# Splitting one weight block over two DMA queues, loading three parameter rows instead of four, and dropping the joining block of a gated SSM and FFN kernel

## Chip, cores and metric

The kernel runs on one core of one Trainium2 chip. The metric is device time in microseconds of one execution, the median of three runs. Engines are named as the profile names them: PE (TensorE matmul, PEld its weight loads), DVE (VectorE), ACT (ScalarE), POOL (GpSimd), SP (SyncE). SP and ACT also issue DMA transfers; SPq and ACTq stand for these issuing instructions.

## The reference

One input x of 2048 rows by 448 columns goes through two branches, which a gate mixes row by row.

```
g   = sigmoid((x * gate_w).sum(-1))
A:    Lam_bar = exp(dt * (Lambda_re + i Lambda_im)),  dt = exp(log_dt)
      B_bar   = ((Lam_bar - 1) / Lam)[:, None] * (B_re + i B_im)
      h_t     = Lam_bar * h_(t-1) + B_bar x_t          (448 complex states)
      y       = 2 Re(C h) + x * Dskip
B:    out     = silu(x @ w1) @ w2                       (448 -> 1792 -> 448)
result = g * y + (1 - g) * out
```

Inputs and output are bfloat16. The parameters Lambda_re, Lambda_im and log_dt are rows of 448 values; the kernel needs them as columns, one value for each partition.

## The kernel before

**Tiles.** Rows of x are taken in pairs (even, odd). With the partition axis for x's columns, x is held transposed in XT: row blocks 0, 1 and 2 of 128 columns each, and a remainder of 64 columns as block 3. W1 lies in W1E in the same four row blocks; the first 768 of its columns come first (FA = 768), further columns later. A step of the first feed-forward product takes 512 even or odd rows and two 128-column blocks of W1 (fb and fb + 1), which fill two PSUM banks. PSUM has eight banks, taken in turn.

**An order written out by hand.** Each operation is handed to a Tracker with the names that it reads and writes. The Tracker appends it to the list of its engine, with waits on other engines' semaphores where needed. Each engine works through its own list strictly in order, so the order of the calls in the source is the order on each engine. DMA transfers are entries of SP's or ACT's list as well. At the end `emit` writes the lists out, inside `nc.Block()`: each engine branches to a block of its own, and at the block's end all engines wait for each other (line 1178 in the profile).

**The opening.** SP and ACT issue in turn (lines 276 to 294): the first half of the columns of XH (512 even rows of x, four pieces XA0 to XA3), W1's row block 0 in two column halves of 384, then on SP W1's row block 1 whole (768 columns, 192 KB), on ACT the second half of XH's columns (256 KB). Then come the four parameter rows, each one partition of R: log_dt and Lambda_re on SP, Lambda_im and Dskip on ACT. W1's row block 2 follows, then the remainder block in two pieces (`ld_wr`), then W1's later columns. SP waits for the two remainder pieces (`T.wait_all("sp", gE)`) before it issues the DMA transposes that bring the rest of x and the B matrices.

PE first runs 22 idle matmuls, then turns XH with `turn_x` (transposes by a matmul with the identity ID into banks 6 and 7). `turned_x` is DVE's copy into XT; the key `XTe0j` names it. `ffn1_first` is a generator that yields between matmuls: for six blocks of W1 (fb in the order 0, 2, 4, 1, 3, 5) it goes through row block 0 (in two halves of 256 rows), 1 and 2. Where it yields, other work for PE is put between. `ffn1_rem` adds the remainder block for two fb and lets ACT apply Silu (`ffn1_act`).

**From rows to columns.** `rd` lets DVE copy 64 columns of R, `mm_cols` turns R by four matmuls with four columns of ID, into bank 7, and DVE copies the result to PV: one column of partitions for each parameter row. DVE and ACT then compute columns from PV in turn (`pact` on ACT, `pts` and `ptt` on DVE): dt, the magnitude mag, the phase fractions phf, fr, f2, sine sn and cosine cs, and the decay factors lr, li, nli, lis, rr. f2 is what POOL and DVE need for the phase tables (`phases`, `phases2`); lr and its kin are needed by the scan of the states. Between the matmuls of row block 1, the columns stand after the second one, and the transposes of x blocks 2 and 3 after the fourth.

**The rest.** PE goes on through the feed-forward steps, the products with B, the second feed-forward product and the output product; DVE does the scans, ACT the activations. The last outputs leave through `yout`, and SP waits for all of them.

Of the kernel before, what the change touches and what calls it, by code (L numbers as in the profile page):

```python
# [7 lines left out]
ALU = mybir.AluOpType  # L8
# [11 lines left out]
D = 448  # L20
# [22 lines left out]
class Tracker:  # L43
# [92 lines left out]
                self.known[eng][g] = g.total  # L136
                self.ops[eng].append(("wait", g.sem, g.total))

    def emit(self, block):
        where = {"sp": block.sync, "act": block.scalar, "pool": block.gpsimd,  # L140
                 "dve": block.vector, "pe": block.tensor}
        for e in self.ENGINES:
            def body(eng, items=self.ops[e]):
                for it in items:
                    if it[0] == "wait":
                        eng.wait_ge(it[1], it[2])  # L146
                    else:
                        it[1](eng).then_inc(it[2], it[3])
            where[e](body)


def gated_mix(nc, A_x, A_Lambda_re, A_Lambda_im, A_B_re, A_B_im, A_C_re, A_C_im, A_log_dt,
              A_Dskip, B_x, B_w1, B_w2, gate_w, out):
    with ExitStack() as ctx:
        E = ctx.enter_context
        T = Tracker(nc, ctx)
# [65 lines left out]
        ps = E(nc.psum_tensor("ps", [128, 8, 512], F32))  # L222
# [13 lines left out]
        def swap_xr(eng, h, odd):  # L236
            hs = slice(h * 512, (h + 1) * 512)
            if odd:
                T.op(eng, lambda e: e.tensor_copy(XR[0:64, hs], XT[64:128, 7, hs]), reads=XO[h][1],
                     writes=[f"XR{h}b"])  # L240
            else:
                T.op(eng, lambda e: e.tensor_copy(XR[64:128, hs], XT[0:64, 3, hs]), reads=XE[h][1],
                     writes=[f"XR{h}a"])

        T.op("dve", lambda e: e.memset(R[:, :], 0.0), writes=["R0", "R1", "R2", "R3", "Rd"])
# [13 lines left out]
        def ld_w(eng, j, f0=0, f1=FA, key=""):  # L259
            ld(eng, W1E[:, j, f0:f1], B_w1[j * 128:(j + 1) * 128, f0:f1], f"W1Ej{j}{key}")  # L260
# [18 lines left out]
            ld_w(eng, 0, 384 * c, 384 * c + 384, c)  # L279
        for k, eng in ((2, "sp"), (3, "act")):  # L280
            ld(eng, XH[:, k, 0:256], x0[:, k, 0:256], XA[k])
        ld_w("sp", 1)
        ld("act", XH[:, :, 256:512], x0[:, :, 256:512], XA[4])
        for i, (eng, v) in enumerate((("sp", A_log_dt), ("sp", A_Lambda_re), ("act", A_Lambda_im), ("act", A_Dskip))):
            ld_row(eng, i, v)
        ld_w("sp", 2)
        gE = [ld_wr(eng, c, False) for c, eng in enumerate(("sp", "act"))]
# [22 lines left out]
        for i, src in enumerate((A_B_re, A_B_im)):  # L310
# [17 lines left out]
             writes=["IOTA"])  # L328
# [3 lines left out]
        SGN = ["SGa", "SGb"]  # L332
# [67 lines left out]

        def wj(fb):
            i, c = fb // 2, fb % 2
            return [f"W1Ej0{c}", "W1Ej1", "W1Ej2"] if i < 3 else ["W1Ed0", "W1Ed2"] if i < 5 else ["W1Ee0", "W1Ee1"]

        def w1(fb):
            return lambda p, j: W1E[p, j, ff(fb) * 128:(ff(fb) + 1) * 128] if j < 3 else \
# [17 lines left out]
        def ffn1_first():  # L424
            banks = [nxt() for _ in range(NF1)]
            for j, h in ((0, 0), (0, 1), (1, None), (2, None)):
                c = slice(0, 512) if h is None else slice(256 * h, 256 * h + 256)
                for n, fb in enumerate((0, 2, 4, 1, 3, 5)):
                    bank = banks[fb]
                    T.op("pe", lambda pe, fb=fb, bank=bank, j=j, h=h, c=c: pe.matmul(  # L430
                        ps[:, bank, c], W1E[:, j, ff(fb) * 128:(ff(fb) + 1) * 128], XT[:, j, c],
                        start=(h == 0), stop=(h == 0), skip_group_check=(h != 0)),
                        reads=[f"W1Ej{j}" if j else f"W1Ej0{fb % 2}"] + (
                            ["XTe02"] if j == 2 else [f"XTe0{j}{h}"] if h is not None else [f"XTe0{j}0", f"XTe0{j}1"]),
                        writes=[f"ps{bank}"])
                    if (j, h, n) in ((0, 0, 3), (0, 0, 5), (1, None, 1), (1, None, 3)):
                        yield
            yield banks

        def ffn1_rem(banks, fb):  # L440
            def mm(pe):
                ins = None
                for i, p in enumerate((LO, UP)):
                    ins = pe.matmul(ps[:, banks[fb + i], :], w1(fb + i)(p, 3), xh(0, 0, 3, p), start=False, stop=True,  # L444
                                    skip_group_check=True)
                return ins
            T.op("pe", mm, reads=rem_ffn1(0, 0, fb), writes=[f"ps{banks[fb]}", f"ps{banks[fb + 1]}"])
            ffn1_act(0, fb, banks[fb], 2)
# [11 lines left out]
                yield  # L460

        def rd():
            T.op("dve", lambda e: e.tensor_copy(R[0:4, D:512], R[0:4, 384:448]), reads=["R0", "R1", "R2", "R3"],  # L463
                 writes=["Rd"])

        def mm_cols(pe):
            ins = None
            for pt in range(4):
                ins = pe.matmul(ps[:, 7, pt * 8:pt * 8 + 4], R[:, pt * 128:(pt + 1) * 128],  # L469
                                ID[:, 0:4], start=True, stop=True)  # L470
            return ins
        ones = nc.const_aps.tensor(1.0, [128, 128], BF16)
# [13 lines left out]
        def turn_x(j, i):  # L486
            def mm(pe):
                ins = None
                for k in (2 * i, 2 * i + 1):
                    ins = pe.transpose(xp[j][:, k * 128:(k + 1) * 128], XH[:, k, j * 128:(j + 1) * 128], ID[:, :])  # L490
# [11 lines left out]
        first = ffn1_first()  # L502
# [5 lines left out]
        turned_x(1, 1)  # L508
        rd()
        next(first)  # L510
        T.op("pe", mm_cols, reads=["R0", "R1", "R2", "R3", "Rd", "ID"], writes=["ps7"])
        T.op("dve", lambda e: e.tensor_copy(
            PV[:, :, :], ps[:, 7, 0:32].rearrange("p (t c) -> p t c", c=8)[:, :, 0:4]),
            reads=["ps7"], writes=["PV"])
        next(first)

        names = {}

# [15 lines left out]
        def pts(o, a, s1, s2, op0, op1, ra):  # L534
            T.op("dve", lambda e: e.tensor_scalar(col(o), a, s1, s2, op0, op1), reads=ra, writes=[o])

        def ptt(o, a, b, op, ra):
            T.op("dve", lambda e: e.tensor_tensor(col(o), a, b, op), reads=ra, writes=[o])

        def pact(o, a, f, ra, scale=1.0, bias=0.0):  # L540
            T.op("act", lambda e: e.activation(col(o), a, f, bias=bias, scale=scale),
                 reads=ra, writes=[o])
# [3 lines left out]
            col("phf"), LIM, 1.0 / TWO_PI, col("dt"), ALU.mult, ALU.mult), reads=["PV", "dt"], writes=["phf"])  # L546
        ptt("ar", col("dt"), LRE, ALU.mult, ["dt", "PV"])
        pact("mag", col("ar"), AF.Exp, ["ar"])
        for j in (2, 3):
            for i in range(2):  # L550
                turn_x(j, i)
        for j in (2, 3):
            turned_x(j)
        T.op("dve", lambda e: e.tensor_copy(XR[64:128, 0:512], xp[3][0:64, :]), reads=["ps7"], writes=["XR0a"])
        T.op("act", lambda e: e.activation(JK[:, 0:1], HP[:, :], AF.Silu), reads=["HP"], writes=["JK0"])
        pts("phr", col("phf"), MAGIC, -MAGIC, ALU.add, ALU.add, ["phf"])
# [6 lines left out]
        T.op("dve", lambda e: e.scalar_tensor_tensor(  # L563
            c1("f2s", 3), c1("f2", 3), -1.0, SG[:, 0:1], ALU.mult, ALU.mult),
            reads=["f2"] + SGN, writes=["f2s"])
        pact("sn", col("fr"), AF.Sin, ["fr"], scale=SIN_SCALE)
        pact("cs", col("afr"), AF.Sin, ["afr", "HP"], scale=-SIN_SCALE, bias=HP[:, 0:1])
        ptt("lr", col("mag"), col("cs"), ALU.mult, ["mag", "cs"])
        ptt("li", col("mag"), col("sn"), ALU.mult, ["mag", "sn"])
        pts("nli", col("li"), -1.0, None, ALU.mult, ALU.bypass, ["li"])  # L570
        T.op("dve", lambda e: e.tensor_tensor(c1("lis", 3), c1("li", 3), SG[:, 0:1], ALU.mult),
             reads=["li"] + SGN, writes=["lis"])
        ptt("rr", col("mag"), col("mag"), ALU.mult, ["mag"])
        first = next(first)


        GP = (0, 0, 1, 1)
# [54 lines left out]
        def skip():  # L632
            for b in range(4):
# [8 lines left out]
        phases(0)  # L642
        phases(2, "dve")
        phases2(0)
        swap_xr("dve", 1, 0)
        phases2(2)
        phases(3)
# [2 lines left out]
             writes=["BTz"] + BTK[2:4])  # L650
# [393 lines left out]
            for _ in range(n):  # L1044
                nxt()

        for fb in (0, 2, 4):
            ffn1_rem(first, fb)
        pair(*ffn1_pair(0, NF1))
        run(ffn1(0, NF1 + 2))  # L1050
        late([ffn1_pair(1, 0)])
# [54 lines left out]
        f = ffn1(2)  # L1106
# [68 lines left out]
            yout(2 * kt + odd, bank, c)  # L1175
        T.wait_all("sp", outs)

        with nc.Block() as block:
            T.emit(block)


def bass_gated_mix__ssm_conv_s5__dense_activation_silu__prompt_kernel(nc, *args):
# [29 lines left out]
```

## Time and profile before

| what | value |
|---|---|
| median of 3 runs | 139.46 us (139.14 to 139.64) |
| the profiled execution's own time | 139.14 us |
| its span, first to last instruction | 137.0 us |
| PE, DVE, ACT busy | 132.8, 114.7, 93.7 us |
| PE's idle time in the opening, by releaser | 0.25 us W1E transfer, 0.38 us DVE's copy to R |
| granted TensorE clock | 1.0 |

The span is shorter than the execution's own time by 2.14 us, which lie before the first and after the last instruction. Times in the profile count from the first instruction. A line of the timeline gives the start, the length, the engine, the source line, the operation, the written and the read tile, and in brackets the idle time before it and what ended it. A matmul's length includes the time in which its results drain, so that lengths of neighbouring matmuls overlap; the distance between starts is what one costs. XT<-XN and the like name the written tile first. XN is the tile that XH is part of.

### The profile page before, as it was taken

Reading aid. Unit: us, or ns where it says so; the run is one execution under the profiler, and the core shown is the slowest. Engines: PE = TensorE matmul, PEld = TensorE weight load, DVE = VectorE, ACT = ScalarE, POOL = GpSimd, SP = SyncE. Lnnn points to the kernel's source line nnn. Section 1 sums busy time; section 2 is a strip of 40 time slices with the busy share of each in tenths; the row PEclk is TensorE's granted clock in tenths of the full one; section 3 lists DMA queues with packets and bytes.
Section 4 is the critical chain, followed back from the end, with each engine's and each line's share of the span. In section 5 each row is a group of like instructions: output and inputs, shape, how many; then the busy total and the mean of one; then the engine's idle time right before and its main releaser. Section 6 shows DMA issues by size and latency. Waiting matters only on the chain.

```text
span 137.0 us, 2417 instructions
## 1 busy us (share of the span) xinstructions
PE 132.8 (97%) x962; PEld 65.1 (48%) x963; DVE 114.7 (84%) x150; ACT 93.7 (68%) x146; POOL 15.3 (11%) x32
## 2 busy tenths in 40 slices
PE   7889999999999999999999999999999999999992
PEld 7444444444444554444445544445555555555551
DVE  1379999374699999999999999999999999990563
ACT  0369798899939994599997996797214437889200
POOL 7108179305000000000000000000000000000000
PEclk9999999999999999999999999999999999999999
DMA  4998949999999130000320000000000000232123
GB/s 112 264 282 168 170 83 164 146 189 370 384 194 139 36 75 0 5 0 0 77 62 20 0 0 0 5 0 0 0 0 0 0 5 20 80 101 67 67 101 101
DMA packets 24897, 11.94 MB, mean 87 GB/s; under 512 B 16564, under 2 KB 24376, under 8 KB 24888
## 3 DMA queue, kind: packets, MB, share of 16 engines
q1 hardware_dynamic: 23140, 10.76, 35.8%
q10 hardware_dynamic: 1748, 1.04, 2.6%
q8 instruction: 7, 0.11, 0.3%
q14 instruction: 2, 0.02, 0.0%
HBM read 5.51 MB, written 1.84 MB: 54 GB/s over the span
## 4 chain that ended last, share of the span: by engine, by line
PE 91%; DMA 3%; DVE 2%; ACTq 2%; issue 0%; DVEq 0%
PE ps L364 42%; PE ps L772 31%; PE ps L994 15%; DMA R<-in_A_Dskip_dram 3%; ACTq L227 2%; PE ps L430 2%; DVE HS L841 1%; DVE TMPS L1018 1%; PE ps L444 1%; PE ps L490 0%; PE ps L469 0%; DVE R L463 0%; DVEq L146 0%
## 5 line engine op out<-in xcount | busy, mean ns | idle before, releaser
L772 PE MATMUL ps<-W,AT 128*128 128x448 bf16 x224 | 42.9, 353 | 0.0
L364 PE MATMUL ps<-XT,W1E 64*128 64x512 bf16 x325 | 40.1, 376 | 0.0
L452 ACT ACTIVATE AT<-ps 128x1024 bf16<-128x1024 f32 x28 | 28.2, 1019 | 9.9 <-PE ps L364 9.8
L772 PEld LDWEIGHTS ps<-W,AT 128*128 128x128 bf16 x224 | 21.7, 98 | 21.2 <-issue 0.4
L364 PEld LDWEIGHTS ps<-XT,W1E 64*128 64x128 bf16 x325 | 16.5, 94 | 20.0 <-ACT VE L803 0.8
L364 PE MATMUL ps<-XT,BT 64*128 64x512 bf16 x156 | 20.2, 376 | 0.1
L785 ACT ACTIVATE BT<-ps,GT 128x448 bf16<-128x448 f32 x8 | 5.1, 633 | 13.1 <-PE ps L772 13.1
L364 PEld LDWEIGHTS ps<-XT,BT 64*128 64x128 bf16 x156 | 8.1, 94 | 9.6 <-DVE HS L841 0.6
L841 DVE SCALAR_TENSOR_TENSOR HS<-VE,P,ps 128x512 bf16<-128x512 bf16 (+1 forms) x13 | 9.6, 781 | 2.6 <-PE ps L364 2.3
L885 DVE TENSOR_TENSOR_SCAN G<-P,Q 128x1024 f32<-128x1024 f32 (+1 forms) x6 | 11.4, 1921 | 0.0
L994 PE MATMUL ps<-CO,VE 128*128 128x448 bf16 (+2 forms) x63 | 11.1, 332 | 0.0
L994 PE MATMUL ps<-CO,HS 128*128 128x448 bf16 x56 | 11.1, 352 | 0.0
L364 PE MATMUL ps<-XR,W1E 64*128 64x512 bf16 x25 | 9.2, 376 | 0.0
L994 PEld LDWEIGHTS ps<-CO,VE 128*128 128x128 bf16 x63 | 6.0, 98 | 4.8
L994 PEld LDWEIGHTS ps<-CO,HS 128*128 128x128 bf16 x56 | 5.5, 98 | 5.1
L838 DVE TENSOR_TENSOR Q<-G,COS 128x2048 bf16<-128x2048 f32 (+1 forms) x4 | 7.0, 1756 | 0.1
L838 DVE TENSOR_TENSOR Q<-G,SIN 128x2048 bf16<-128x2048 f32 (+1 forms) x4 | 7.0, 1752 | 0.0
L805 ACT ACTIVATE ps<-VE,P 128x1024 f32<-128x1024 bf16 x6 | 6.7, 1119 | 0.2
L841 DVE SCALAR_TENSOR_TENSOR VE<-HS,P,FP 128x512 bf16<-128x512 bf16 (+1 forms) x7 | 6.6, 977 | 0.1
L1018 DVE SCALAR_TENSOR_TENSOR OT<-ps,GT,BT 128x448 bf16<-128x448 f32 x4 | 2.6, 682 | 4.8 <-PE ps L994 4.8
L803 ACT ACTIVATE VE<-ps 128x1024 bf16<-128x1024 f32 x6 | 6.1, 1018 | 0.8 <-PE ps L364 0.8
L841 DVE SCALAR_TENSOR_TENSOR FP<-HS,P,VE 128x1024 f32<-128x1024 bf16 (+1 forms) x4 | 6.2, 1551 | 0.1
(120 smaller groups left out, 170.5 us busy)
## 6 DMA issues: line engine op xcount, KB each, us to landing
W<-in_B_w_dram SPq DMA_DIRECT2D x1, 1568.0 KB, 9.1
XN<-in_A_x_dram SPq DMA_DIRECT2D x1, 896.0 KB, 5.1
out_dram<-OT SPq DMA_DIRECT2D x8, 112.0 KB, 1.7
out_dram<-TMPS SPq DMA_DIRECT2D x7, 112.0 KB, 1.7
HS<-HS SPq DMA_DIRECT2D x4, 128.0 KB, 2.5
W1E<-in_B_w_dram SPq DMA_DIRECT2D x2, 192.0 KB, 4.1
XN<-in_A_x_dram SPq DMA_DIRECT2D x1, 384.0 KB, 5.9
XN<-in_A_x_dram ACTq DMA_DIRECT2D x1, 256.0 KB, 4.6
```

The source lines that it names most:

```text
L227: return T.dma(eng, lambda e: e.dma_start(dst, src), writes=[key], group=group)
L364: ins = pe.matmul(ps[:, bank, :], w(p, j), xh(odd, h, j, p), start=start and j == js[0], stop=stop and j == js[-1], skip_group_check=seeded)
L452: T.op("act", lambda e: e.activation(a[:, fb:fb + n, :], ps[:, bank:bank + n, :], AF.Silu), reads=[f"ps{bank + i}" for i in range(n)], wri ...
L772: ins = pe.matmul(ps[:, bank, 0:D], a[:, fb, q * 128:(q + 1) * 128], W2[:, ff(fb), :], start=(first and fb == 0), stop=(fb == NFB - 1), sk ...
L785: T.op("act", lambda e: e.activation(bs(tile), ps[:, bank, 0:D], AF.Copy, scale=sc), reads=[f"ps{bank}", "GT2" if h else "GRI"], writes=ks)
L803: T.op("act", lambda e: e.activation(VE[:, m:m + 2, hs], ps[:, b[0]:b[0] + 2, :], AF.Copy), reads=[f"ps{i}" for i in b], writes=vs)
L805: T.op("act", lambda e: e.activation(ps[:, o[0]:o[0] + 2, :], VE[:, m:m + 2, hs], AF.Copy, scale=c1("lr", pt)), reads=vs + ["lr"], writes= ...
L838: T.op("dve", lambda e: e.tensor_tensor(o, a, b, op), reads=reads, writes=writes)
L841: T.op("dve", lambda e: e.scalar_tensor_tensor(o, a, s, b, ALU.mult, ALU.add), reads=reads, writes=writes)
L885: T.op("dve", lambda e: e.tensor_tensor_scan(G[:, c, w], rb, Q1[:, c, w], init, ALU.mult, ALU.add), reads=[f"Q1{c}", "rr", f"G{c}"], write ...
L994: ins = pe.matmul(ps[:, bank, c], state(kt, odd, m), CO[:, m, c], start=False, stop=(m == YB[-1]), skip_group_check=True)
L1018: T.op("dve", lambda e: e.scalar_tensor_tensor(o, ps[:, bank, c], g, bs(tile)[:, c], ALU.mult, ALU.add), reads=[f"ps{bank}", "GT1_1", f"BS ...
```

## The change

The change has four parts.

- W1's second row block (j = 1) is loaded as two halves of 384 columns, one issued by SP and one by ACT, in the place where SP issued it whole. Matmuls wait for the half that they read. The generator now yields once in this block, after three matmuls (fb 0, 2, 4).
- Dskip's row is no longer loaded into R, so the parameter columns come from three rows. The column matmuls write to columns 256 and up of bank 7 under a name of their own (pv); DVE's copy to PV reads pv and ps7. The transposes of x blocks 2 and 3 follow directly, and DVE's copy of block 2 stands ahead of the parameter arithmetic.
- The remainder matmuls of fb 0, 2 and 4 with their Silu are moved up, so that on ACT sine and cosine stand behind the second Silu. The decay columns lr, li, nli and lis become `decays()`, called behind `phases2(0)`.
- `emit` writes the instructions without `nc.Block()`.

```diff
-    def emit(self, block):
-        where = {"sp": block.sync, "act": block.scalar, "pool": block.gpsimd,
-                 "dve": block.vector, "pe": block.tensor}
+    def emit(self):
+        nc = self.nc
+        where = {"sp": nc.sync, "act": nc.scalar, "pool": nc.gpsimd, "dve": nc.vector, "pe": nc.tensor}
         for e in self.ENGINES:
...
-        ld_w("sp", 1)
+        for c, eng in enumerate(("sp", "act")):
+            ld_w(eng, 1, 384 * c, 384 * c + 384, c)
         ld("act", XH[:, :, 256:512], x0[:, :, 256:512], XA[4])
-        for i, (eng, v) in enumerate((("sp", A_log_dt), ("sp", A_Lambda_re), ("act", A_Lambda_im), ("act", A_Dskip))):
+        for i, (eng, v) in enumerate((("sp", A_log_dt), ("sp", A_Lambda_re), ("act", A_Lambda_im))):
             ld_row(eng, i, v)
...
-                    if (j, h, n) in ((0, 0, 3), (0, 0, 5), (1, None, 1), (1, None, 3)):
+                    if (j, h, n) in ((0, 0, 3), (0, 0, 5), (1, None, 2)):
                         yield
...
-            T.op("dve", lambda e: e.tensor_copy(R[0:4, D:512], R[0:4, 384:448]), reads=["R0", "R1", "R2", "R3"],
+            T.op("dve", lambda e: e.tensor_copy(R[0:3, D:512], R[0:3, 384:448]), reads=["R0", "R1", "R2"],
                  writes=["Rd"])
...
-                ins = pe.matmul(ps[:, 7, pt * 8:pt * 8 + 4], R[:, pt * 128:(pt + 1) * 128],
+                ins = pe.matmul(ps[:, 7, 256 + pt * 8:260 + pt * 8], R[:, pt * 128:(pt + 1) * 128],
                                 ID[:, 0:4], start=True, stop=True)
...
-        T.op("pe", mm_cols, reads=["R0", "R1", "R2", "R3", "Rd", "ID"], writes=["ps7"])
+        T.op("pe", mm_cols, reads=["R0", "R1", "R2", "Rd", "ID"], writes=["pv"])
         T.op("dve", lambda e: e.tensor_copy(
-            PV[:, :, :], ps[:, 7, 0:32].rearrange("p (t c) -> p t c", c=8)[:, :, 0:4]),
-            reads=["ps7"], writes=["PV"])
-        next(first)
+            PV[:, :, :], ps[:, 7, 256:288].rearrange("p (t c) -> p t c", c=8)[:, :, 0:4]),
+            reads=["pv", "ps7"], writes=["PV"])
+        for j in (2, 3):
+            for i in range(2):
+                turn_x(j, i)
+        turned_x(2)
...
         pact("mag", col("ar"), AF.Exp, ["ar"])
-        for j in (2, 3):
-            for i in range(2):
-                turn_x(j, i)
-        for j in (2, 3):
-            turned_x(j)
+        turned_x(3)
...
+        first = next(first)
+        ffn1_rem(first, 0)
+        ffn1_rem(first, 2)
         pact("sn", col("fr"), AF.Sin, ["fr"], scale=SIN_SCALE)
         pact("cs", col("afr"), AF.Sin, ["afr", "HP"], scale=-SIN_SCALE, bias=HP[:, 0:1])
-        ptt("lr", col("mag"), col("cs"), ALU.mult, ["mag", "cs"])
-        ptt("li", col("mag"), col("sn"), ALU.mult, ["mag", "sn"])
-        pts("nli", col("li"), -1.0, None, ALU.mult, ALU.bypass, ["li"])
...
+        ffn1_rem(first, 4)
+
+        def decays():
+            ptt("lr", col("mag"), col("cs"), ALU.mult, ["mag", "cs"])
+            ptt("li", col("mag"), col("sn"), ALU.mult, ["mag", "sn"])
+            pts("nli", col("li"), -1.0, None, ALU.mult, ALU.bypass, ["li"])
...
         ptt("rr", col("mag"), col("mag"), ALU.mult, ["mag"])
-        first = next(first)
...
         phases(0)
         phases(2, "dve")
         phases2(0)
+        decays()
         swap_xr("dve", 1, 0)
...
-        for fb in (0, 2, 4):
-            ffn1_rem(first, fb)
         pair(*ffn1_pair(0, NF1))
...
-        with nc.Block() as block:
-            T.emit(block)
+        T.emit()
```

More of the change, by code (lines that the diff above doesn't have):

```diff
@@ L137, in wait_all @@
                 self.ops[eng].append(("wait", g.sem, g.total))
-    def emit(self, block):
-        where = {"sp": block.sync, "act": block.scalar, "pool": block.gpsimd,
-                 "dve": block.vector, "pe": block.tensor}
+    def emit(self):
+        nc = self.nc
+        where = {"sp": nc.sync, "act": nc.scalar, "pool": nc.gpsimd, "dve": nc.vector, "pe": nc.tensor}
         for e in self.ENGINES:
[L143 to L149, printed above, removed]
+            eng = where[e]
+            for it in self.ops[e]:
+                if it[0] == "wait":
+                    eng.wait_ge(it[1], it[2])
+                else:
+                    it[1](eng).then_inc(it[2], it[3])
 def gated_mix(nc, A_x, A_Lambda_re, A_Lambda_im, A_B_re, A_B_im, A_C_re, A_C_im, A_log_dt,
@@ L243, in swap_xr @@
                      writes=[f"XR{h}a"])
-        T.op("dve", lambda e: e.memset(R[:, :], 0.0), writes=["R0", "R1", "R2", "R3", "Rd"])
+        T.op("dve", lambda e: e.memset(R[:, :], 0.0), writes=["R0", "R1", "R2", "Rd"])
         T.op("dve", lambda e: e.memset(SG[0:64, 0:1], -1.0), writes=["SGa"])
@@ L402, in wj @@
             i, c = fb // 2, fb % 2
-            return [f"W1Ej0{c}", "W1Ej1", "W1Ej2"] if i < 3 else ["W1Ed0", "W1Ed2"] if i < 5 else ["W1Ee0", "W1Ee1"]
+            return [f"W1Ej0{c}", f"W1Ej1{c}", "W1Ej2"] if i < 3 else ["W1Ed0", "W1Ed2"] if i < 5 else ["W1Ee0", "W1Ee1"]
         def w1(fb):
@@ L432, in ffn1_first @@
                         start=(h == 0), stop=(h == 0), skip_group_check=(h != 0)),
-                        reads=[f"W1Ej{j}" if j else f"W1Ej0{fb % 2}"] + (
+                        reads=[f"W1Ej{j}" if j > 1 else f"W1Ej{j}{fb % 2}"] + (
                             ["XTe02"] if j == 2 else [f"XTe0{j}{h}"] if h is not None else [f"XTe0{j}0", f"XTe0{j}1"]),
                         writes=[f"ps{bank}"])
-                    if (j, h, n) in ((0, 0, 3), (0, 0, 5), (1, None, 1), (1, None, 3)):
+                    if (j, h, n) in ((0, 0, 3), (0, 0, 5), (1, None, 2)):
                         yield
@@ L565, in gated_mix @@
             reads=["f2"] + SGN, writes=["f2s"])
+        first = next(first)
+        ffn1_rem(first, 0)
+        ffn1_rem(first, 2)
         pact("sn", col("fr"), AF.Sin, ["fr"], scale=SIN_SCALE)
         pact("cs", col("afr"), AF.Sin, ["afr", "HP"], scale=-SIN_SCALE, bias=HP[:, 0:1])
-        ptt("lr", col("mag"), col("cs"), ALU.mult, ["mag", "cs"])
-        ptt("li", col("mag"), col("sn"), ALU.mult, ["mag", "sn"])
-        pts("nli", col("li"), -1.0, None, ALU.mult, ALU.bypass, ["li"])
-        T.op("dve", lambda e: e.tensor_tensor(c1("lis", 3), c1("li", 3), SG[:, 0:1], ALU.mult),
-             reads=["li"] + SGN, writes=["lis"])
+        ffn1_rem(first, 4)
[3 more added lines that the diff above has]
+            pts("nli", col("li"), -1.0, None, ALU.mult, ALU.bypass, ["li"])
+            T.op("dve", lambda e: e.tensor_tensor(c1("lis", 3), c1("li", 3), SG[:, 0:1], ALU.mult),
+                 reads=["li"] + SGN, writes=["lis"])
         ptt("rr", col("mag"), col("mag"), ALU.mult, ["mag"])
-        first = next(first)
         GP = (0, 0, 1, 1)
```

## The prediction

> **What bounds the kernel now.** I read the page first, then the busy time by stage, then PE's timeline of the opening, then the chain of waits, and last what the closing line of the program leaves behind. The page, busy time by engine:
>
> ```profile
> span 137.0 us, 2417 instructions
> ...
> PE 132.8 (97%) x962; PEld 65.1 (48%) x963; DVE 114.7 (84%) x150; ACT 93.7 (68%) x146; POOL 15.3 (11%) x32
> ```
>
> PE has some 4 us without work. The table by stage (length; busy time and instructions of each engine; clock; DMA share) says where:
>
> ```profile
> 0.00:3.90 3.90, 3.08 (x28) 2.87 (x28) 0.71 (x6) 0.00 (x0) 2.93 (x10) 1.00 0.50 124
> 3.90:10.10 6.20, 5.39 (x42) 2.84 (x43) 3.10 (x16) 3.48 (x7) 0.22 (x2) 1.00 0.99 282
> 10.10:31.40 21.30, 21.30 (x199) 9.56 (x200) 17.27 (x27) 18.89 (x20) 10.74 (x13) 1.00 0.93 160
> ...
> 33.00:134.00 101.00, 101.00 (x681) 49.07 (x682) 91.30 (x100) 70.02 (x118) 0.28 (x2) 1.00 0.23 54
> 134.00:137.00 3.00, 0.52 (x8) 0.31 (x5) 0.90 (x2) 0.00 (x0) 0.00 (x0) 1.00 0.27 81
> ```
>
> From 10.1 to 134 PE is full at full clock, so a change can move the time only by letting that stream begin earlier or later, by tearing a hole in it, or by shortening what follows it. The edits lie before 10.1 and after the last output. PE's timeline of the opening (start, length, last the idle time before):
>
> ```profile
> 5.11 0.83 PE L430 MATMUL ps<-XT,W1E 128*128 128x256 bf16 x6
> 6.19 0.61 PE L430 MATMUL ps<-XT,W1E 128*128 128x512 bf16 x2 [0.25 <-DMA W1E<-in_B_w_dram]
> 7.17 0.24 PE L469 MATMUL ps<-ID,R 128*128 128x4 bf16 x4 [0.38 <-DVE R L463]
> 7.49 0.38 PE L430 MATMUL ps<-XT,W1E 128*128 128x512 bf16 x1
> 7.71 0.61 PE L490 MATMUL ps<-ID,XN 128*128 128x128 bf16 x8
> 8.15 2.00 PE L430 MATMUL ps<-XT,W1E 128*128 128x512 bf16 x8
> ```
>
> Durations here include the pipeline's tail; I count starts. A 512-column matmul costs 0.215 us (starts at 10.09, 10.31, 10.53), a 256-column one 0.11, a transpose 0.055, the four column matmuls 0.1 together. So the six of row block 0 are done at 5.77 and PE is empty until 6.19: 0.42 us for W1's second row block. Two matmuls last to 6.62, and PE is empty until 7.17: 0.55 us for the parameter rows. Two more matmuls (7.27 to 7.70, one record is missing), eight transposes to 8.15, eight matmuls to 9.87; the remainder starts at 10.09, so another 0.22 us is lost, 0.12 of it before row block 2, whose transposed x is copied by DVE only from 8.13 to 8.55. The chain of waits agrees on which wait ends last:
>
> ```profile
> 3.33 3.44 DMA R<-in_A_Dskip_dram
> 6.78 0.04 DVEq L146
> 6.81 0.05 issue
> 6.86 0.18 DVE R L463
> 7.04 0.14 issue
> 7.17 0.24 PE ps L469 x4
> ```
>
> The binding event is the landing of the last parameter row at 6.77, and the column matmuls follow it by 0.40. The last view is the instructions of the line that closes the block:
>
> ```profile
> L1178 SPq COMPARE_BRANCH  x1: 33/33/33, 136.6 to 136.6; - x1
> L1178 SPq DRAIN  x1: 13/13/13, 136.8 to 136.8; - x1
> ...
> L1178 PEldq EVENT_SEMAPHORE  x1: 51/51/51, 136.9 to 136.9; - x1
> ```
>
> The last output is issued at 134.98 and takes 1.5 us, so it is there at about 136.5; the rest of the span, from 136.6 to 137.0, is branch, drain and the engines' mutual wait.
>
> **The change, part by part.**
>
> *No joining block.* Removed: the entry branch of each engine and, at the end, 136.6 to 137.0. The span loses 0.39 us if nothing takes its place; nothing hides it, since SP arrives last. The trace does not show what follows the span (139.14 against 137.0, so 2.14 us around it). Bounds: 0, if that time grows by what the span loses; 0.42, with some hundredths for the entry branches; no instruction is added that could make it a loss. I take 0.39, because the row shows it on the latest engine.
>
> *W1's second row block in halves.* The 192 KB piece is issued on SP at 2.17 and read by PE at 6.19. The halves are issued at 2.17 (SP) and 2.20 (ACT). Pieces of 96 KB took 2.4 and 2.6 us to land on these two queues, which gives 4.6 to 4.8; the latest I allow is the present 6.19. PE wants the first half at 5.77. Three matmuls instead of two now stand ahead of the column matmuls and need that half alone. By 4.8 they run from 5.77 to 6.42, by 6.19 to 6.84; both are before the column matmuls can start with the rows as they land now (7.17). So the 0.42 us wait disappears into the wait for the rows: alone this part moves one matmul, 0.215 us, ahead of the wait.
> The Trainium skill speaks against this part: DMA: Bandwidth & Descriptors, section "Issuing engines are not separate DMA queues", has transfers of all issuing engines interleave on the same 16 DMA engines, so a second queue saves only issue time. The DMA share of 0.99 from 3.9 to 10.1 agrees that there is no spare bandwidth; by that rule the half comes no sooner than 6.19, and the sum below would not change.
>
> *Three rows instead of four.* Dskip's row, the one that lands last, is gone, but Lambda_im stays on ACT and gets a new place: ahead of it are now XH1, W1's two halves, XH3 and the 256 KB of x (576 KB instead of 480 KB). ACT's issues cost 0.41 to 0.46 us each, so Lambda_im is issued at about 3.15, where it was 2.70 and Dskip 3.33. SP has 96 KB less ahead of its two rows. On both queues together the bytes ahead are the same 896 KB, on engines that are full. The nearest row is thus Dskip's landing: T = 6.77. Earlier bound: T = 6.02, below which PE is not free (6.42). Later bound: the 256 KB of x, issued at 2.66 instead of 2.20, land 4.6 us later (the page's figure for that transfer) at 7.26, and W1's third row block, issued at 3.30, passes them and the row as well (192 KB at the stage's 282 GB/s, 0.7 us): T = 7.95.
>
> *The order behind the columns.* Let M = max(6.42, T + 0.40) be the start of the column matmuls. Then 0.1 for them, four transposes of x column block 2 to M + 0.32. Block 3 shares bank 7 with the columns, and the copy to PV reads that bank: it starts 0.28 after M (7.45 against 7.17), lasts 0.18, and with about 0.07 for the signal PE goes on at M + 0.53 (a new stall of 0.21, where a matmul stood before). Four transposes to M + 0.75, three matmuls to M + 1.40, six of row block 2 to M + 2.69; DVE's copy for them, now ahead of the parameter arithmetic, ends at about M + 0.95, so the 0.12 goes. With the 0.10 before the remainder: M + 2.79, against 10.09 - 7.17 = 2.92 now. Gain 0.13 at T = 6.77; 0.88 at 6.02; a loss of 1.05 at 7.95. The time changes by T's change one to one.
>
> *Moves at no cost.* Sine and cosine behind two Silu: ACT's first Silu then waits only for PE; PE needs its banks 1.52 us after the remainder starts (11.61 against 10.09), and PE's own 0.22 plus tail 0.2 plus 1.0 of Silu leaves 0.1. Without the move the cosine (10.17 to 10.47) would hold it, at up to the front's gain. The four decay columns (0.9 + 3 x 0.15) behind the first phase table: first read by ACT at 26.5, ten us later. ACT's queue gets 0.45 of issuing and loses 0.24: its table load moves from 5.54 to 5.75, the Exp that needs it starts at 7.66, cover 0.6. SP issues as many transfers as before, but its six x transposes and the others begin when both remainder pieces of W1 have landed (7.88). If ACT's piece comes 0.2 later, all of them do, the copy at 28.14 too:
>
> ```profile
> DVE XR L239 <- DMA XT<-in_A_x_dram: 3.1, 1, 3.1
> ```
>
> It ends at 28.43 and PE reads it at 28.87: cover 0.3 less what the front gains, so 0 for the forecast and at most 0.2.
>
> **Sum.** 0.39 + 0.13 = 0.52. The profiled execution took 139.14, the fastest of three; the median is 139.46. Against its own time it gives 138.62, against the median 138.94. I predict the median. Differences within 0.3%, 0.42 us, are about what a measurement of this kernel can tell from no change.
>
> **Rivals.**
> - *One of the two gains fails.* Either the exit is only passed on to the time around the span (gain 0.13, 139.33), or the block's 0.39 is real and T is 6.95 (front -0.05, gain 0.34, 139.12), or the transposes take back 0.1 to 0.2. For it: the two gains lie just above 0.42 together, and each has zero within its bounds. Against it: the closing line's rows, and a row fewer to wait for. Middle 139.2.
> - *Lambda_im behind the large x transfer: slower.* PE's order is fixed, so row block 1's second half, all transposes and row block 2 are queued behind the column matmuls, and they behind the one row that lands last. Price: T beyond 6.77 one to one. From T = 7.29 on (6.77 + 0.13 + 0.39) it eats the whole gain; a T of 7.75 gives 139.46 - 0.52 + 0.98 = 139.92, the bound 7.95 gives 140.12. For it: the issue of x 0.46 later, and 96 KB more in front on that queue. Against it: SP's queue is that much lighter and engines serve both.
> - *The rows come early.* If T follows the SP rows' position, T is at or below 6.3 and the front gains 0.6 or more: 139.46 - 0.39 - 0.6 = 138.47. For it: Lambda_im stood ahead of Dskip on its queue and must have landed before it.
>
> **How the numbers follow.** Forecast 0.42, early rows 0.10, one gain failing 0.33, Lambda_im late 0.15. Faster by over 0.3% is the first two, 0.52; within it the third; slower the last. The range: low 138.5, near the early rows; high 139.6, past the middle rival and into the beginning of the late row, which leaves some 0.1 on either side. The likeliest case's own range is 138.7 to 139.04 (T from 6.5 to the point where the gain is 0.42).
>
> **What would show it.** Right: no instructions of the closing line after the last output, and a span that ends at its landing; the copy to R between 6.6 and 7.1, the first remainder matmul near 9.96, PE full from there, and no wait for W1 at row block 1. Wrong: a DVE wait before the copy to R that lasts past 7.3; a hole in PE at 28.9 with a DMA as its releaser; a hole at 11.6 before the banks of the first Silu; or the time around the span well over 2.14 us.

## The result and the profile after

The changed kernel takes 138.26 us (median of 15 runs, 137.78 to 139.60), the kernel before 139.29 in its own 15 runs (138.94 to 140.37). The ratio is 0.9937, with a 95% interval from 0.9912 to 0.9962: shorter, clear of noise, but by under 1%. Between the medians it is 1.03 us; by the ratio 0.88, with an interval from 0.53 to 1.23. The forecast was a gain of 0.52 and a time of 138.94 in a range from 138.5 to 139.6, so the direction was right and the time lies 0.24 us below the range. Of the 0.68 between 138.94 and 138.26, 0.17 is not the change's: the kernel before took 139.29 here and 139.46 in the three runs that the forecast started from. The profiled execution took 137.81 us, one of the two shortest of the 15; the profile of before, at 139.14, was near the low end too.

The head of its page and the busy time by engine:

```profile
span 136.3 us, 2407 instructions
...
PE 133.2 (98%) x962; PEld 66.0 (48%) x963; DVE 113.7 (83%) x150; ACT 93.5 (69%) x146; POOL 16.9 (12%) x32
```

Between the two profiled executions the span is 0.7 us shorter, but the time is 1.33 us shorter (139.14 to 137.81): what lies around the span went from 2.14 to 1.51 us. That is where the forecast missed. The table by stage (length; busy time and instructions by engine in the order PE, PEld, DVE, ACT, POOL; clock; DMA share) shows the stream behind the opening as it was, without a hole:

```profile
3.90:10.10 6.20, 6.08 (x42) 3.71 (x44) 3.24 (x17) 3.39 (x6) 0.22 (x2) 1.00 0.93 277
10.10:31.40 21.30, 21.30 (x200) 9.51 (x198) 16.31 (x25) 18.93 (x21) 12.97 (x16) 1.00 0.91 171
```

PE's timeline of the opening (start, length; no line carries a wait):

```profile
5.67 1.67 PE L430 MATMUL ps<-XT,W1E 128*128 128x256 bf16 x9
7.18 0.24 PE L469 MATMUL ps<-ID,R 128*128 128x4 bf16 x4
7.28 0.81 PE L490 MATMUL ps<-ID,XN 128*128 128x128 bf16 x8
8.14 1.89 PE L430 MATMUL ps<-XT,W1E 128*128 128x512 bf16 x8
9.96 0.39 PE L444 MATMUL ps<-XT,W1E 64*128 64x512 bf16 x1
```

The first matmul of the remainder starts at 9.96, exactly where the forecast put it, but by another way. The rows had landed early: DVE copies them at 6.12 (the forecast: 6.6 to 7.1).

```profile
6.12 0.16 DVE L463 COPY R<-R 3x64 bf16<-3x64 bf16 x1
```

PE could not use it. The same four 256-column matmuls start at 4.01 in both profiles; the transposes behind them start at 4.45 before and at 4.82 after:

```profile
4.01 0.60 PE L430 MATMUL ps<-XT,W1E 128*128 128x256 bf16 x4
4.45 0.28 PE L490 MATMUL ps<-ID,XN 128*128 128x128 bf16 x2
```

```profile
4.01 1.01 PE L430 MATMUL ps<-XT,W1E 128*128 128x256 bf16 x4
4.82 0.42 PE L490 MATMUL ps<-ID,XN 128*128 128x128 bf16 x2
```

From start to start a 256-column matmul takes 0.21 us in the changed kernel, from 4.2 until about 6.1, and 0.11 behind that; in the kernel before it takes 0.11 from 4.01 on. So PE ran at half rate until about 6 here. The clock column of the stage table reads 1.00 in both profiles all the same; the half rate is read from the starts. So row block 0 ended at 6.53 instead of 5.77, and the column matmuls, behind three more matmuls, began at 7.18, limited by PE. An early landing and a slow PE cancelled: that the remainder began at 9.96 is luck. The chain that ended last has this stretch so:

```profile
5.88 1.46 PE ps L430 x9
7.34 0.08 PE ps L469 x4
7.42 0.24 PE ps L490 x4
7.67 0.02 issue
7.69 0.40 PE ps L490 x4
```

The piece from 7.42 to 7.69 is the stall at bank 7: the fifth transpose starts 0.24 after the start of the fourth, where 0.055 is usual.

At the end, the last output lands at 136.25 and the span ends at 136.30. Before, it landed at 136.52, and branch, drain and the mutual wait lasted to 136.99. So within the span the closing line cost 0.47, and 0.05 is left of it: 0.42 us, the upper bound of the forecast.

### The profile page after: what moved, and what is told of

It reads as the page before. It is cut to its first block, busy times and chain, and to the rows that moved or that the text cites. A ratio compares the mean times of both kernels' runs of the same rounds, so it can differ in the third digit from the quotient of the medians.

```text
span 136.3 us, 2407 instructions
## 1 busy us (share of the span) xinstructions
PE 133.2 (98%) x962; PEld 66.0 (48%) x963; DVE 113.7 (83%) x150; ACT 93.5 (69%) x146; POOL 16.9 (12%) x32
## 4 chain that ended last, share of the span: by engine, by line
PE 96%; DVE 2%; issue 0%; DVEq 0%
PE ps L364 43%; PE ps L778 31%; PE ps L1000 15%; PE ps L430 4%; PE ps L478 2%; PE ps L490 1%; DVE HS L847 1%; DVE TMPS L1024 1%; PE ps L444 1%; PE ps L469 0%; DVEq L146 0%
```

## Experiments

In all sixteen kernels the sixteen transfers that transpose x, B and C on their way are replaced by plain transfers of the same bytes from about 7.9 us on: that transposition is left out, and other values reach the later matmuls. Everything that the change touches is kept. The time around the span is a run's time less the span of that same run, which is on record to 0.1 us; medians are over all runs, ranges in brackets. "Ratio to before" compares with runs of the real kernel before on the same chip.

### What the joining block is worth

Four kernels: both openings, each with and without the block.

```
plain_block:    before, plain transfers        plain_noblock: the same, with
-        with nc.Block() as block:             plain_opening: changed opening, block kept
-            T.emit(block)                     plain_after:   changed kernel, plain transfers
+        T.emit()
```

> The kernel before, in which the 16 transposing transfers (of x, B and C, from 7.9 us on) are plain transfers of as many bytes into the same tiles; so x, B and C lie untransposed there and the values are others. It is the base of the following kernels, which all have plain transfers. Both theories: within 0.4 us of before, since PE is the bound from 10.1 us on and these transfers begin only when the opening is nearly over; 2.1 us around the span.

> The base with one edit: the instructions are written without the joining block. Theory 1 (the joining block is dearer than its 0.39 us in the span, because the time around the span falls too, from 2.14 to 1.5): about 1.0 us faster than the base, with 1.5 us around the span. Theory 2 (the block is worth its 0.39 us, and the rest of the gain comes from parameter rows that land early): 0.4 us faster, with 2.1 us around the span.

> The opening of the changed kernel, with the joining block left in, and plain transfers. Theory 1: within 0.3 us of the base, 2.1 us around the span. Theory 2: 0.6 us faster than the base.

> The changed kernel with plain transfers, on the chip of the other three. Both theories: 0.9 to 1.1 us faster than the base. In its profile, theory 1 has the moment at which matmuls go from 0.107 to 0.055 us each (3.9 us in the run of before, 5.9 in that of after) at another place again, and the remainders starting earlier or later by up to 0.9 us with it.

| kernel | time, us | span | around | ratio to before [95%] |
|---|---|---|---|---|
| plain_block | 138.89 (138.51 to 139.31) | 137.05 | 1.90 | 0.9935 [0.9906, 0.9965] |
| plain_noblock | 138.11 (137.73 to 138.48) | 136.6 | 1.50 | 0.9874 [0.9827, 0.9922] |
| plain_opening | 138.56 (138.26 to 138.94) | 136.6 | 2.02 | 0.9904 [0.9871, 0.9937] |
| plain_after | 137.88 (137.61 to 138.05) | 136.35 | 1.54 | 0.9858 [0.9806, 0.9910] |

From plain_block to plain_after it is 1.01 us, as between the two real kernels (1.03), so the stand-ins carry the effect. The block is worth 0.78 with the old opening and 0.68 with the new one, and the runs of neither pair overlap. The opening is worth 0.33 with the block and 0.23 without it, but there the runs of both pairs overlap. The forecast had 0.39 and 0.13. The time around the span falls by 0.40 and 0.48 when the block goes: the half that the forecast did not have. The plain transfers alone take the kernel before from 139.77 on that chip to 138.89, more than the 0.4 that I had allowed.

### What of the block costs time outside the span

First the mutual wait without the branches:

```
+        nc.all_engine_barrier()      # after T.emit(), in the changed kernel
```

> The changed kernel with plain transfers and one mutual wait of all engines at the end, but without the block's branches. So far the block costs 0.4 us in the span and about 0.5 us in the time around it. Theory A (the mutual wait is what is paid for, in both places): 0.6 to 0.9 us slower than plain_after_2, with 1.9 to 2.1 us around the span. Theory B (the branches pay for the time around the span): the span grows by 0.2 to 0.4 us, the time around it stays at 1.5, 0.2 to 0.4 slower.

> The changed kernel with plain transfers once more, the common measure of this set. The copy to R starts in its profile where the last parameter row lands; this was 6.12 in the run of after and 6.99 in plain_after. If the landing is as loose as that, it lies somewhere between 6.0 and 7.2 again, and the remainders start 2.8 us after the column matmuls whatever it is.

It gives the gain back: 138.71 (138.38 to 139.03, ratio 0.9929 [0.9907, 0.9950]) against 137.87 (137.72 to 137.93) for the changed kernel on another chip, with 2.08 around the span against 1.52. So outside the span it is the wait of the engines for each other and not the branches. Inside it, 0.30 us lie between the last output's landing (136.60) and the span's end (136.90) in plain_join's profile, 0.46 to 0.47 in the three profiles with the block and its branches. Its closing line in plain_join's profile (engine, instruction, durations in ns, first and last start):

```profile
L1185 POOLq EVENT_SEMAPHORE  x2: 17/17/17, 136.7 to 136.8; - x2
L1185 POOLq DRAIN  x1: 299/299/299, 30.3 to 30.3; - x1
...
L1185 SPq DRAIN  x1: 7/7/7, 136.7 to 136.7; - x1
```

GpSimd drains at 30.3 and then waits over 106 us for SyncE. Without the wait it could go on to whatever follows the program. The next kernels have no barrier; instead, named engines also wait for all outputs, so that they end late.

```
         T.wait_all("sp", outs)
+        T.wait_all("pool", outs)     # or "pe", "dve", "act", or several
```

> The changed kernel with plain transfers; no block and no mutual wait, but ACT, POOL, DVE and PE also wait for all outputs as their last step, as SP does. If the time around the span grows because all engines end late (what follows the program on each engine then can't run beside SP's wait), it is 2.0 us around, the span within 0.1 of plain_after_2's 136.35: 138.3 to 138.4, 0.5 slower. If it is the mutual wait's own signals that cost, 1.5 around and no difference: 137.9.

> As the last, but PE alone waits for all outputs beside SP. If what follows on any one engine is as long, 2.0 us around the span like with all engines; if PE's part is short or another engine's decides, 1.5 to 1.6 around and about 137.9.

> The changed kernel with plain transfers, and ScalarE alone also waits for all outputs before it ends. Theory 1 (each engine's own closing work after the program runs beside the last wait of SyncE when the engine ends early, and the latest one decides): the time around the span goes from 1.5 to between 1.6 and 1.8 us, like TensorE's 1.75, and the total from about 137.9 to 138.1 to 138.4. Theory 2 (only TensorE has closing work that counts, and the other engines cost only when they end with it): 1.5 and 137.9. Theory 3 (any engine that ends late costs the whole half microsecond): 2.05 and 138.4 or more.

> The changed kernel with plain transfers, and VectorE alone also waits for all outputs before it ends. Theory 1 (closing work of each engine, the latest decides): 1.6 to 1.8 us around the span. Theory 2 (TensorE alone counts): 1.5. Theory 3 (any late engine costs all of it): 2.05.

> The changed kernel with plain transfers, and GpSimd alone also waits for all outputs before it ends. GpSimd has been without work since about 31 us, so its closing work has the longest time to run early. Theory 1: 1.6 to 1.8 us around the span. Theory 2 (TensorE alone counts): 1.5. Theory 3 (any late engine costs all of it): 2.05. If none of the three engines alone moves it and all together make 2.13, the closing work shares something that is used by one engine after the other.

> The changed kernel with plain transfers, and ScalarE, VectorE and TensorE also wait for all outputs before they end; GpSimd ends early, at its last work near 31 us. Alone, GpSimd's late end gave 2.04 us around the span, TensorE's 1.75, VectorE's 1.73, ScalarE's 1.64, none 1.52. Theory 1 (the closing work of the engines runs side by side and the longest that begins late decides): 1.75 to 1.85 around, total near 138.2. Theory 2 (the closing works add up: 0.12 + 0.21 + 0.23): 2.05 to 2.1, total near 138.5.

| ends with SyncE | around the span | time, us | ratio to before [95%] |
|---|---|---|---|
| none (plain_after_2) | 1.52 (1.51 to 1.53) | 137.87 | 0.9871 [0.9848, 0.9895] |
| ScalarE | 1.64 (1.60 to 1.67) | 138.07 | 0.9897 [0.9869, 0.9926] |
| VectorE | 1.73 (1.69 to 1.76) | 138.15 | 0.9904 [0.9877, 0.9931] |
| TensorE | 1.75 (1.72 to 1.82) | 138.36 | 0.9896 [0.9852, 0.9939] |
| these three | 1.87 (1.83 to 1.94) | 138.50 | 0.9923 [0.9896, 0.9950] |
| GpSimd | 2.04 (2.02 to 2.06) | 138.43 | 0.9918 [0.9882, 0.9954] |
| all four | 2.13 (2.09 to 2.21) | 138.74 | 0.9930 [0.9902, 0.9957] |

Nothing of this shows in the page. Here is the head of late_pool's, and then plain_after's:

```profile
span 136.4 us, 2417 instructions
```

```profile
span 136.4 us, 2407 instructions
```

Equal spans, and 0.50 us between the times around them. Each engine that ends late costs something around the span: ScalarE 0.12, VectorE 0.21, TensorE 0.23, GpSimd 0.52. GpSimd alone accounts for most of the 0.61 of all four, which I had not expected of any one engine. The three others together cost 0.35, more than the largest of them (0.23) and less than their sum (0.56), so neither a pure "longest decides" nor a pure sum fits; late_three missed both windows that I had written, the first by 0.02, and late_pe fell between its two.

The rows come from three chips, but the base hardly differs between them: kernels in which SyncE alone ends last have 1.54 (sine_early) on the chip of ScalarE's, VectorE's and GpSimd's rows and 1.48 (fill_2) on that of the three together. The column of times also holds what the opening did in those runs; in the three kernels in which TensorE ends late the span is some 0.25 longer as well (136.60 against 136.35).

A second measure leaves the opening out: the profiled execution's time less the start of the remainder's first matmul (plain_after_2: 137.72 less 9.90). It is 127.81 to 127.85 in nine profiles without block or join in which SyncE alone ends last (in a tenth, rows_on_sp, 128.12), and 127.98 when ScalarE ends late too, 128.08 VectorE, 128.10 TensorE, 128.23 these three, 128.40 GpSimd, 128.53 all four: the same order as in the table.

What the engines do there is in no trace. That each has closing work of its own, longest on GpSimd, which is over before SyncE's last wait when the engine ends early, is an inference from this table and not shown. The Trainium skill, in Runtime: NRT & Kernel Launch, section "The ~15µs preamble/postamble breakdown", states a closing wait for all engines of about 1.5 us; the 1.5 here also holds what precedes the span, so no run here confirms or contradicts that figure, and the page says nothing of the order in which the engines end.

### The three parts of the opening

```
plain_whole   W1's second row block whole on SP:   +        ld_w("sp", 1)
plain_rows4   four rows again, Dskip's last:       +  ("act", A_Lambda_im), ("act", A_Dskip)
rows_on_sp    the third row on SP:                 +  ("sp", A_Lambda_im)
```

> The changed kernel with plain transfers, W1's second row block whole on SP again; three rows, the new order and no block stay. Theory 'the rows decide' (as the prediction had it): the first matmul of row block 1 goes back to about 6.2, but Lambda_im has only 480 KB ahead of it on its queue and lands at about 6.6, so the column matmuls start at 6.9 to 7.0: within 0.15 us of plain_after_2. Theory 'the weights decide': 0.3 to 0.4 us slower, the wait that the halves took away.

> The changed kernel with plain transfers, with Dskip's row loaded, copied and turned as a fourth one; halves, order and no block stay. Theory 'the rows decide': the last row lands 0.1 to 0.25 us later (in before Dskip landed 0.2 after Lambda_im), and the time is longer by as much. Theory 'the clock decides' (PE is still at half speed or behind when the rows land, so their landing has slack): no difference beyond 0.1.

> The changed kernel with plain transfers; Lambda_im is the third row on SP instead of the only one on ACT. If the queue position decides when a row lands (SP's rows landed last at 6.2 and 6.4 in two profiles, ACT's at 6.7 and 6.9), the column matmuls start at 6.6 to 6.8 and the time is 0.2 to 0.4 us shorter than plain_after_2, 137.5 to 137.7. If the engines' whole load decides, no difference beyond 0.1.

plain_whole takes 138.07 (138.00 to 138.20, ratio 0.9888 [0.9865, 0.9911]), 0.2 above the changed kernel, and the ranges hardly touch (137.61 to 138.05 and 137.72 to 137.93). That lies between the two expectations. PE does not wait for W1 there; in its profile the last row lands at 7.08, not near 6.6, and PE waits for that:

```profile
5.63 1.48 PE L431 MATMUL ps<-XT,W1E 128*128 128x256 bf16 x9
7.48 0.24 PE L470 MATMUL ps<-ID,R 128*128 128x4 bf16 x4 [0.38 <-DVE R L464]
```

So the halves are worth about 0.2, and not through an earlier W1; whether through earlier rows, one profile cannot say, since 7.08 is a landing that the changed opening also shows. The halves themselves came hardly sooner than the whole piece. From issue to landing (KB, us), first in the changed kernel's profile, then in that of the kernel before:

```profile
W1E<-in_B_w_dram SPq DMA_DIRECT2D x1, 96.0 KB, 4.2
W1E<-in_B_w_dram ACTq DMA_DIRECT2D x1, 96.0 KB, 4.4
```

```profile
W1E<-in_B_w_dram SPq DMA_DIRECT2D x1, 192.0 KB, 4.0
```

The first half lands at 6.39 in the changed kernel's profile and at 5.62 to 6.33 in the fifteen others that have halves (mean of all 5.93), the whole piece at 6.07 to 6.14. So the prediction's 4.6 to 4.8, taken from pieces of 96 KB that were issued at 1.24, did not hold for pieces issued at 2.17. The rule of the Trainium skill that the prediction weighs there (DMA: Bandwidth & Descriptors, section "Issuing engines are not separate DMA queues"), by which a second queue saves only issue time, came nearer. In the changed kernel's profile it cost nothing, since PE reached row block 1 at 6.53.

plain_rows4 takes 138.37 (137.69 to 138.57, ratio 0.9903 [0.9879, 0.9927]): 0.5 more, with one of its six runs as short as the changed kernel's. Its Lambda_im lands at 6.66 and its Dskip at 7.26, and the column matmuls begin at 7.66, exactly 0.40 behind that. The fourth row is what lands last, as the prediction had it:

```profile
7.66 0.24 PE L471 MATMUL ps<-ID,R 128*128 128x4 bf16 x4 [0.33 <-DVE R L465]
```

rows_on_sp takes 137.99 (137.49 to 138.59, ratio 0.9868 [0.9825, 0.9911]): no gain. In its profile, which is that of its longest run (138.59), the rows land at 6.81, and PE then waits for the large x transfer instead:

```profile
7.97 0.62 PE L492 MATMUL ps<-ID,XN 128*128 128x128 bf16 x8 [0.52 <-DMA XN<-in_A_x_dram]
```

### The stall at bank 7, and sine and cosine

```
fill, fill_2: the last three matmuls of row block 1 between the transposes of x's blocks 2 and 3
-        for j in (2, 3):
-            for i in range(2):
-                turn_x(j, i)
+        for i in range(2):
+            turn_x(2, i)
         turned_x(2)
+        next(first)
+        for i in range(2):
+            turn_x(3, i)
sine_early: sn and cs ahead of the first two Silu, as in the kernel before
+        pact("sn", ...); pact("cs", ...)
         ffn1_rem(first, 0)
```

> The changed kernel with plain transfers; the last three matmuls of row block 1 stand between the transposes of x block 2 and those of block 3, so that PE works while DVE's copy to PV holds bank 7. By the prediction's count the remainders start 2.58 us after the column matmuls instead of 2.79: 0.2 us faster than plain_after_2, 137.65. Rival: the copies of x block 3 come later in turn and the remainder waits for them: no difference.

> The changed kernel with plain transfers, and the last three matmuls of W1's row block 1 put between the transposes of x's third and fourth column block, once more beside the kernel before. If the 0.2 us that the bank's stall costs are gained when PE is at full clock: 0.15 to 0.2 below the changed kernel's 137.88, so 137.70. If the rows' landing and the clock decide the front: 137.8 to 137.95.

> The changed kernel with plain transfers, but sine and cosine are back ahead of the first two Silu on ScalarE, as the kernel before has them. If the move was needed (the prediction: the cosine would hold the first Silu by up to the front's gain), TensorE shows a hole near 11.6 us of up to 0.3 us that ScalarE ends, and the total is 0.1 to 0.3 above 137.9. If the banks are early enough, there is no hole and the total is 137.9 within 0.1.

fill puts the remainder 2.58 us behind the column matmuls in both of its profiles, against 2.78 or 2.79 in the changed order: the stall is gone, as counted. But the times are 137.80 (137.63 to 137.94) and 137.89 (137.76 to 138.07), ratios 0.9856 [0.9817, 0.9896] and 0.9889 [0.9839, 0.9939], against 137.87 and 137.88 for the changed kernel. In both profiles the rows landed late (7.13 and 7.03, column matmuls at 7.53 and 7.43), and nothing that fill moves lies ahead of these. For fill the profiled run was also the longest of the six. Whether the late landings are chance is open; a better kernel it is not shown to be.

sine_early takes 137.95 (137.92 to 138.06, ratio 0.9891 [0.9864, 0.9918]), the changed kernel's time within 0.1. ScalarE's timeline there:

```profile
10.06 0.19 ACT L546 ACTIVATE P<-P 128x4 f32<-128x4 f32 x1
10.15 0.28 ACT L546 ACTIVATE P<-P,HP 128x4 f32<-128x4 f32 x1
10.52 2.85 ACT L454 ACTIVATE AT<-ps 128x1024 bf16<-128x1024 f32 x3
```

The cosine ends at 10.43, in time that ScalarE has free, and the first Silu starts at 10.52, the same start as with the move (plain_after):

```profile
10.52 1.94 ACT L454 ACTIVATE AT<-ps 128x1024 bf16<-128x1024 f32 x2 [0.37 <-PE ps L446]
```

## Why the prediction missed, step by step

**The joining block: the step that failed.** The span loses 0.42 in the profiles, as the prediction read from the closing line's rows. The term failed in the sentence on what the trace does not show: 2.14 us around the span, bounded by "0, if that time grows by what the span loses; 0.42". I allowed that this time might grow and not that it might shrink. It shrank by 0.4 to 0.5, so the term is 0.7 to 0.8 instead of 0.39. "No instruction is added that could make it a loss" argued one side only. The same view of the kernel before has rows that the prediction did not weigh: GpSimd drains at 33.1 and then stands still for over 103 us, in which it could do something else.

```profile
L1178 POOLq EVENT_SEMAPHORE  x2: 17/17/17, 136.8 to 136.9; - x2
L1178 POOLq DRAIN  x1: 296/296/296, 33.1 to 33.1; - x1
```

The rival "the exit is only passed on to the time around the span" was the wrong way round.

**The opening: right in its form, and in its size as far as the runs can tell.** Between the column matmuls and the remainder the count was exact: 2.78 or 2.79 in fourteen profiles of the changed order (rows_on_sp, which waits for x, has 3.26) against 2.91 or 2.92, a gain of 0.13. That the time changes by the start of the remainder one to one is shown too: in the nine profiles named behind the table of late ends this start runs from 9.90 to 10.45, and the time behind it stays within 0.04. By medians the opening gave 0.23 to 0.33, but with runs that overlap. By the start of the remainder it gave 0.10: 10.17 on average in the three profiles of the old opening, 10.07 in the twelve of the changed one (fill's two, with another order, left out). So a gain above 0.13 is not shown. T, the landing of the last row, was taken as unchanged at 6.77. Three profiles of the old opening have 6.73, 6.78 and 7.06 (mean 6.86); fourteen of the new one have 5.95 (the changed kernel itself) and 6.33 to 7.13 (mean 6.80). That supports "unchanged" on the average, and a spread of over 1 us hides a shift of 0.2. Of the parts, the fourth row is worth 0.5 and the halves 0.2 when undone alone, more than the whole opening. One profile suggests why: with four rows in the changed opening (plain_rows4) the last one lands at 7.26, some 0.4 later than in the old opening, and leaving the row out gives about that back. That the larger queue ahead of Lambda_im makes the 0.4 is worked out and not shown.

**M = max(6.42, T + 0.40).** The second term held wherever PE waited for the copy (7.48, 7.66 above). The first did not: with the half rate of the changed kernel's profile PE was free at 7.18, not 6.42. That is no exception: in six of those twelve profiles PE was the later of the two, in plain_opening at 6.94 although it ran at full rate from 5.2 on. The 6.42 came from one profile with early x.

**Moves at no cost.** No hole at 11.6 and none at 28.9: PE is busy for 21.30 of the 21.30 us from 10.1. ("From 10.1 to 134 PE is full" passes over 31.4 to 33.0, where PE has 1.52 of 1.60 us before and 1.53 after.) But "without the move the cosine would hold" the first Silu was wrong, as sine_early shows; the move was worth nothing that the runs show.

**Rivals.** The time 138.26 lies near "the rows come early" (138.47), whose cause the runs do not support: T's average did not move. "Lambda_im late" did not come about; no profile of the changed opening has T past 7.13, and 7.29 was needed to lose the whole gain as I had sized it.

**The sum again.** With 0.73 for the block (the mean of 0.78 and 0.68) and 0.28 for the opening (the mean of 0.33 and 0.23) it is 1.01, against 1.03 measured. Of the 0.49 that was missing against 0.52, 0.34 is the block's; the other 0.15 falls to the opening by these medians, and is within their noise.

## What to carry to other kernels

A closing join of all engines had two prices here: 0.42 us behind the last output, and 0.4 to 0.5 us outside the span, which goes when the other engines, GpSimd above all, may end early. So compare times and not spans when an exit changes. Where the trace is blind, the bound must be open on the gaining side too. The landing of a small transfer behind large ones (DMA share 0.93 to 0.99) is a distribution, and a profile before and a profile after are two draws from it.

## What had not been expected of the hardware

- The time around the span depends on which engines end late: 1.5 us when only SyncE does, 2.04 with GpSimd beside it, 2.13 with all.
- The moment from which PE ran at full rate (0.055 us from start to start for 128 columns, 0.107 until then) lay before 4.1 us of the span in sine_early's profile and at 6.9 in plain_join's, both with the changed opening and the same idle matmuls ahead; the clock column reads 1.00 throughout. The Trainium skill, TensorE: Matmul & The Clock Gate, Part 1, has a free-running window of about 3.4 us and a transition that varies by 0.5 us; the spread here is nearly 3 us.
- A one-row transfer of 0.9 KB behind the bulk landed anywhere from 5.95 to 7.13 us in profiles of the same opening.
- Replacing the sixteen transposing transfers, all behind the opening, by plain ones took 0.9 us off the kernel before and narrowed its runs to 0.8 us.
